# Position bias in whole groups of 16 rows on TensorE, its relus made two groups ahead

## The chip, the cores and the metric

The kernel runs on one core of a Trainium2 chip. The metric is device time in microseconds, the median of several executions. Beside it stands one execution that the hardware profiler recorded: its trace gives the rows below. The engines are called by the profile's names: PE multiplies matrices, PEld loads PE's weights, DVE (vector), ACT (activation) and POOL work elementwise, SP issues most of the transfers.

## The reference, cut to what matters

Attention over 4 batches of 8 heads, 576 positions of 64 features, with a position bias that a small network of 32 hidden units makes; its output goes through two feed-forward stages.

```
scores = q @ k.T / sqrt(64)
rel    = pos[:, None] - pos[None, :]
x      = log1p(|rel|) / log1p(max(pos[:, None], 1))
bias   = relu(x * w1 + b1) @ w2            # one value per head, i and j
attn   = softmax(scores + bias)
x1     = leaky(attn @ v reshaped @ w_in) @ w_out
out    = a routed mixture of 8 experts over x1
```

The bias is the same for all batches. It is 8 x 576 x 576 values, each a sum over 32 hidden units.

## The kernel before

Three phases follow each other. The first one holds the attention, the feed-forward's first product and the position bias, and is the one that the change is in. Its instructions are written in one order and a scheduler then places them on the engines' queues; each engine takes its queue strictly in that order.

**The bias.** A row i of the bias depends on j only through |i - j|, so 16 rows make a group: group m covers rows 16m to 16m+15, and there are 36 groups. `bias_relu` makes for one group four tiles `mk`, one for each q from 0 to 3; each holds 4 rows x 32 hidden units on the 128 partitions and up to 576 distances along the free side. The table `RELU` says for each whether ACT (L222) or DVE (L224) makes it. `bias_units` multiplies each `mk` with the coefficients `cf` (made on POOL, L254) into its own strip of 32 PSUM partitions, `tile_position=(0, 32 * q)` (L270): 4 rows x 8 heads. Four such matmuls, one for each q, are a piece; the 591 columns of a group (576 and 15 for the skewed layout) are cut where the distance turns round and where a PSUM bank ends, two or three pieces in all. Then the strips are copied to the tile `bt` (by ACT, L70, or DVE, L78), and SP writes `bt` to the DRAM tensor `bias` (L284). Up to group 11 and from group 32 on (`both`), all pieces of a group lie in one PSUM tile of the pool `psS`, and one copy takes them; between, each piece has a PSUM tile of the pool `psM`. Both pools have two buffers.

A PE matmul of fp32 data stands in the trace as two records, so a whole piece shows as x8 and a whole group of two pieces as x16; the timeline merges neighbours of one tile under the first one's shape.

**Around it.** `bias_units` is a generator. `phase1` first takes 32 units of it (called the prelude here: groups 0 to 15, with the first loads and conversions of q and k between them), and then the rest comes from a `Filler` between the parts of the first eight attention steps. A step is 128 rows of q of two heads: `scores` (PE L413, then DVE L418, which adds the bias), `exps` (ACT L426), `normalise` (POOL, ACT or DVE, L435 to L444), `transposes` (PE L464, L486) and, at a group's end, `values` (PE L500). From step 8 on the filler gives `up_units` (PE L525, tile `psh`), whose weights `wi` come out of DVE's conversions of `w_in` (`w_t`, L99 to L107, then L78 and L82), spread over the steps from 2 on. Later steps load the bias back from DRAM (`prob<-bias`), and further conversions (`wo_t`) prepare `w_out`.

The filler takes units while a debt is positive, and each unit names its price in ns:

```
quota = 40 * 800.0 / 6.5 if n < 8 else ...
...
fl.run(quota / 2)     # twice in each step
```

Of the kernel before, what the change touches and what calls it, by code (L numbers as in the profile page):

```python
# [38 lines left out]
BC = S + 15  # L39
BP = 608  # L40
# [10 lines left out]

RELU = ("DDAD", "DADD", "DAAD", "ADDA")

WIDE, RELU_BUFS, BIAS_BUFS, COEF_M = 12, 11, 5, 2

PROBS = 4

# [11 lines left out]
def copy_act(nc, out, in_):  # L69
    nc.scalar.activation(out=out, in_=in_, func=AF.Copy)  # L70
# [143 lines left out]
def bias_relu(nc, e, m, qs):  # L214

    out = []
    n = max(16 * m + 16, S - 16 * m)
    for q in qs:
        mk = e.bout.tile([128, S], F32, tag="mk", name="mk", bufs=RELU_BUFS)
        o, x, k = mk[:, :n], e.lw[:, :n], slice(4 * m + q, 4 * m + q + 1)  # L220
        if RELU[m % 4][q] == "A":
            nc.scalar.activation(out=o, in_=x, func=AF.Relu, bias=e.bv[:, k])  # L222
        else:
            nc.vector.tensor_scalar(out=o, in0=x, scalar1=e.bv[:, k], scalar2=0.0, op0=ALU.add, op1=ALU.max)  # L224
        out.append(mk)
    return out


def bias_pieces(m, o):


    c0 = 16 * m + 16
    out = []
    for a, z, d, falls in ((0, c0, c0 - 1, True), (c0, BC, 1, False)):
        while a < z:
            b = min(z, a + 512 - (a + o) % 512)
            out.append((a, b, d, falls))
            d += a - b if falls else b - a
            a = b
    return out  # L240


def bias_units(nc, e, wide):

    nm = S // 16
    nxt = bias_relu(nc, e, 0, range(4))
    for m in range(nm):  # L250
        mk, nxt = nxt, []
        if m % COEF_M == 0:
            cf = e.bout.tile([128, 4 * COEF_M, 4 * H], F32, tag="cf", name="cf", bufs=2)
            nc.gpsimd.tensor_tensor(  # L254
                out=cf, in0=e.coef.rearrange("p g h -> p (g h)").unsqueeze(1).to_broadcast([128, 4 * COEF_M, 4 * H]),
                in1=e.br[:, 4 * m:4 * m + 4 * COEF_M].unsqueeze(2).to_broadcast([128, 4 * COEF_M, 4 * H]), op=ALU.mult,
            )
        bt = e.bout.tile([128, BC], F32, tag="bt", name="bt", bufs=BIAS_BUFS)
        both = m < wide or m >= 32
        o = 0 if m < 4 else 1024 - BC if m >= 32 else 496 - 16 * m  # L260
        pieces = bias_pieces(m, o)
        if both:
            ps2 = e.psS.tile([128, 2, 512], F32, tag="s", name="psb2").rearrange("p a j -> p (a j)")
        half = (len(pieces) + 1) // 2
        for hf in range(2):
            for a, b, d, falls in pieces[half * hf:half * hf + half]:
                ps = ps2[:, o + a:] if both else e.psM.tile([128, 512], F32, tag="m", name="psb")
                for q in range(4):
                    x = mk[q][:, d - (b - a) + 1:d + 1][:, ::-1] if falls else mk[q][:, d:d + b - a]
                    nc.tensor.matmul(  # L270
                        ps[32 * q:32 * q + 32, :b - a], lhsT=cf[:, 4 * (m % COEF_M) + q], rhs=x,
                        start=True, stop=True, tile_position=(0, 32 * q),
                    )
                if not both:
                    (copy_act if hf or m % 2 else copy_dve)(nc, bt[:, a:b], ps[:, :b - a])
            if m + 1 < nm:
                nxt += bias_relu(nc, e, m + 1, (2 * hf, 2 * hf + 1))
            if hf == 1:
                if both:
                    copy_act(nc, bt, ps2[:, o:o + BC])  # L280

                r0 = 16 * (m % 8) * BP
                dst = e.bias_d[m // 8][:, r0:r0 + 16 * (BP + 1)].rearrange("h (r c) -> r h c", c=BP + 1)
                nc.sync.dma_start(out=dst[:, :, :BC], in_=bt)  # L284
            yield 800


class Attention:
# [274 lines left out]
def phase1(ctx, tc, e):  # L563

    nc = tc.nc
# [22 lines left out]
    for k, g in enumerate(groups):  # L588
        b, hf, p = g
# [7 lines left out]
        if hf == 0 and k >= 2:  # L597
            m = n0 - 4 if b == 0 else start[b - 1, 1, p] + 3
# [21 lines left out]

    bias_setup(nc, e)
    bu = bias_units(nc, e, WIDE)
    for k in range(32):
        if k == 20:
            for g in groups[:2]:
                at.q_load(g)
                at.q_hi(g)
                at.q_lo(g)
            for p in range(2):
                at.kv_load(0, p)  # L630
                at.kv_hi(0, p)
                at.k_lo(0, p)
                at.v_load(0, p)
        next(bu)
# [25 lines left out]
    for n, st in enumerate(steps):  # L660
        g = st[:3]
        b, hf, p = g
# [723 lines left out]
def program(tc, e):  # L1386
# [4 lines left out]
    with ExitStack() as top:  # L1391
# [16 lines left out]
        for n, b in (("const", 1), ("big", 1), ("small", 4), ("raw", 1), ("kvp", 1), ("ptp", 1)):  # L1408
            setattr(e, n, pool(wide, n, b, side="right"))
        e.psS, e.psT = (pool(wide, n, 2, space=PSUM) for n in ("psS", "psT"))  # L1410
        tail = phase1(up, tc, e)
        wide.close()

# [60 lines left out]
```

## Time and profile before

| | us |
|---|---|
| median of 3 runs | 1026.42 (1024.62 to 1027.13) |
| the profiled execution, its time | 1025.94 |
| its span (first to last instruction) | 1024.1 |
| PE busy | 980.9 (96%) |
| DVE busy | 680.3 (66%) |
| ACT busy | 545.1 (53%) |
| the 640 records of L270 (position bias on PE), busy | 61.8, from 6.8 to 104 us |

The shares are means over the whole span; the bias stage, the first tenth of it, has its own. Times inside the trace count from the span's start. Busy time of PE is the union of modelled lengths, and a matmul's modelled end lies a little behind the next one's start. The page's "PEclk" is the clock that TensorE was granted, 1.00 for 2.4 GHz and 0.50 for 1.2 GHz.

### The profile page before, as it was taken

To read this page: it belongs to the slowest core of one execution; us is meant where nothing else is said; L and a number is where in the kernel's file an instruction comes from. 1 tells how busy PE (TensorE), PEld (TensorE's weight loads), DVE (VectorE), ACT (ScalarE), POOL (GpSimd) and SP (SyncE) were. 2 spreads that over 40 slices of the span, in tenths; PEclk is the share of its full clock that TensorE was granted. 3 is DMA by queue.
4 is the path that set the end of the run, shared out by engine and by line. 5 is a ranking of instruction groups with operands and counts; after the bars stand their busy time and mean duration, and the time that the engine had idled before them with its cause. 6 is when DMAs were issued, how large, how long until landed. Compare 5 with 4: busy or idle time off the path is not lost.

```text
span 1024.1 us, 19091 instructions
## 1 busy us (share of the span) xinstructions
PE 980.9 (96%) x6294; PEld 807.3 (79%) x6294; DVE 680.3 (66%) x1719; ACT 545.1 (53%) x1102; POOL 101.4 (10%) x112
## 2 busy tenths in 40 slices
PE   5899999999999999999999999999998999999995
PEld 2345778988889988999888888888877888888884
DVE  8888998979865677667766776669983255313312
ACT  5778777546766666555553333344462455424422
POOL 3332421000000000000000000001002111111110
PEclk8999999999999999999999999999999999999998
DMA  7868889989765566545285633437505157312410
GB/s 246 263 201 248 254 282 305 317 269 288 221 205 146 160 188 211 157 141 164 68 259 170 196 113 103 124 117 235 142 21 216 49 198 275 121 42 92 164 41 23
DMA packets 137602, 180.16 MB, mean 176 GB/s; under 512 B 19842, under 2 KB 89858, under 8 KB 137363
## 3 DMA queue, kind: packets, MB, share of 16 engines
q1 hardware_dynamic: 115554, 149.31, 47.4%
q10 hardware_dynamic: 18576, 19.03, 5.3%
q0 software_dynamic: 3360, 10.49, 3.1%
q8 instruction: 52, 0.85, 0.3%
q14 instruction: 60, 0.48, 0.2%
HBM read 196.18 MB, written 43.94 MB: 234 GB/s over the span
## 4 chain that ended last, share of the span: by engine, by line
PE 59%; issue 18%; DMA 12%; DVE 8%; POOL 2%; ACT 1%; SPq 0%; POOLq 0%; DVEq 0%; ACTq 0%
PE psx L784 19%; PE psh L525 15%; PE pss L413 7%; PE psv L500 7%; DMA out_dram<-o,sidx 6%; PE pst L464 5%; PE psb L270 4%; DMA wo_raw<-in_w_out_dram 2%; DVE mk L224 1%; DMA qraw<-in_q_dram 1%; DMA prob<-bias 1%; DVE prob L418 1%; PE psx L486 1%; POOL xg L1241 1%; POOL prob L444 1%
## 5 line engine op out<-in xcount | busy, mean ns | idle before, releaser
L525 PE MATMUL psh<-x,wi 128*128 128x256 f32 (+1 forms) x1536 | 226.8, 298 | 1.7 <-DVE hst L532 1.7
L525 PEld LDWEIGHTS psh<-x,wi 128*128 128x128 f32 x1536 | 211.7, 190 | 3.7 <-DVE hst L532 3.1
L426 ACT ACTIVATE prob<-prob,stat 128x576 f32<-128x576 f32 x144 | 111.3, 773 | 66.4 <-DVE stat L418 55.8
L418 DVE CUSTOM_DVE_ANT_0 prob<-pss,prob 128x576 f32<-128x576 f32 x144 | 107.8, 751 | 22.8 <-PE pss L413 18.7
L784 PE MATMUL psx<-woh,gh 128*128 128x512 f32 x288 | 113.1, 393 | 0.7 <-ACT gh L70 0.7
L784 PE MATMUL psx<-wol,gh 128*128 128x512 f32 x288 | 112.6, 391 | 0.0
L784 PE MATMUL psx<-woh,gl 128*128 128x512 f32 x288 | 112.2, 390 | 0.0
L82 DVE TENSOR_TENSOR htl<-pt,hth 128x512 fp32r<-128x512 f32 x40 | 25.8, 686 | 127.4 <-ACT hth L70 127.4
L70 ACT ACTIVATE gh<-g 128x512 fp32r<-128x512 f32 x72 | 45.4, 632 | 116.4 <-PE psx L784 102.1
L464 PE MATMUL pst<-ident,prob 128*128 128x128 f32 x576 | 89.7, 278 | 4.9 <-DVE pth L78 2.5
L464 PEld LDWEIGHTS pst<-ident,prob 128*128 128x128 f32 x576 | 66.3, 140 | 23.3 <-issue 13.1
L413 PE MATMUL pss<-kt,qhi 128*128 128x288 f32 x256 | 81.7, 334 | 0.0
L1241 POOL DMA_INDIRECT xg<-x,gidx x22 | 23.5, 1067 | 557.6 <-DMA ws<-in_mw_dram 549.0
L270 PE MATMUL psb<-mk,cf 128*32 128x79 f32 (+49 forms) x640 | 61.8, 426 | 12.7 <-POOL cf L254 6.8
L413 PE MATMUL pss<-kt,qlo 128*128 128x288 f32 x256 | 72.6, 298 | 0.0
L500 PE MATMUL psv<-pth,vs 128*64 128x256 f32 (+1 forms) x512 | 71.5, 413 | 0.0
L801 DVE SCALAR_TENSOR_TENSOR junk<-x1s,en 128x512 bf16<-128x512 f32 x96 | 66.0, 687 | 3.5 <-DMA en<-en_d 2.5
L1272 PE MATMUL pu<-w1h,xh 128*128 128x512 f32 x160 | 65.0, 406 | 0.3 <-ACT xh L70 0.3
L70 ACT ACTIVATE pth<-pst 128x512 f32<-128x512 f32 (+1 forms) x100 | 54.5, 549 | 20.1 <-PE pst L464 12.3
L1303 PE MATMUL pd<-w2h,hth 128*128 128x512 f32 x160 | 62.6, 391 | 1.0 <-ACTq L1228 1.0
L784 PEld LDWEIGHTS psx<-woh,gh 128*128 128x128 f32 x288 | 54.1, 188 | 11.8 <-ACT gh L70 1.0
L1272 PE MATMUL pu<-w1l,xh 128*128 128x512 f32 x160 | 63.3, 396 | 0.0
(224 smaller groups left out, 1862.4 us busy)
## 6 DMA issues: line engine op xcount, KB each, us to landing
ws<-in_mw_dram SPq DMA_DIRECT2D x164, 512.0 KB
prob<-bias SPq DMA_DIRECT2D x64, 288.0 KB
g<-h SPq DMA_DIRECT2D x72, 256.0 KB
prob<-bias SPq DMA_DIRECT2D x64, 256.0 KB
bias<-bt SPq DMA_DIRECT2D x36, 295.5 KB
h<-hst ACTq DMA_DIRECT2D x64, 160.0 KB
w_raw<-in_w_in_dram SPq DMA_DIRECT2D x16, 512.0 KB
h<-hst ACTq DMA_DIRECT2D x64, 128.0 KB
```

What stands on the lines that cost most here:

```text
L70: nc.scalar.activation(out=out, in_=in_, func=AF.Copy)
L270: nc.tensor.matmul(ps[32 * q:32 * q + 32, :b - a], lhsT=cf[:, 4 * (m % COEF_M) + q], rhs=x, start=True, stop=True, tile_position=(0, 32 * q),)
L413: nc.tensor.matmul(ps[:, jh, :288], lhsT=lhsT, rhs=kt[:, c0 + 288 * jh:][:, :288], start=(k == 0), stop=(k == len(ops) - 1),)
L418: nc.vector.tensor_tensor_reduce(out=prv, in0=ps[:, :, :288], in1=prv, scale=-0.125, scalar=3.0e38, op0=ALU.add, op1=ALU.min, accum_out=st ...
L426: nc.scalar.activation(out=pr[:, h], in_=pr[:, h], func=AF.Exp, bias=stat[:, 0, h:h + 1], scale=-1.0, accum_out=stat[:, 1, h:h + 1],)
L464: nc.tensor.transpose(ps[:, 128 * c:128 * c + 128], pr[:, h, 64 * h + 128 * c:][:, :128], e.ident)
L500: nc.tensor.matmul(ps[64 * h:64 * h + 64, :n], lhsT=vs[:, c, h], rhs=ph[:, h, c, :n] if c < 4 else pt[:, :n], start=(c == 0), stop=(c == 4 ...
L525: nc.tensor.matmul(ps[:, :n], lhsT=w[:, kc], rhs=x[:, kc, :n], start=(k == 0), stop=(k == 3 * KD - 1),)
L784: nc.tensor.matmul(ps, lhsT=a[:, c % 4], rhs=w[:, c], start=(k == 0), stop=(k == 3 * KF - 1))
L801: nc.vector.scalar_tensor_tensor(out=junk, in0=x1, scalar=1.0, in1=e.en[:, k], op0=ALU.mult, op1=ALU.mult, accum_out=e.dots[:, t, k:k + 1],)
L1272: nc.tensor.matmul(ps, lhsT=a[:, k], rhs=w[:, k, c], start=(i == 0), stop=(i == 3 * KD - 1))
L1303: nc.tensor.matmul(ps, lhsT=a[:, k], rhs=w[:, k], start=(k == 0 and j == 0), stop=(k == 7 and j == 2))
```

## The change

A unit of `bias_units` is a whole group now and is priced at 1600 ns, where it was half of the pieces at 800 ns; the prelude takes 16 units where it took 32, and the loads of q and k stand before the same group, the tenth. The four relus of a group are written as one block, two groups ahead of their matmuls: groups 0 and 1 before the loop, group m+2 behind the matmuls of group m. Before, they were written in two pairs, one behind each half of the group ahead. Eleven buffers for `mk` become 14.

```
--- before.py
+++ after.py
@@ -51,7 +51,7 @@
 
 RELU = ("DDAD", "DADD", "DAAD", "ADDA")
 
-WIDE, RELU_BUFS, BIAS_BUFS, COEF_M = 12, 11, 5, 2
+WIDE, RELU_BUFS, BIAS_BUFS, COEF_M = 12, 14, 5, 2
 
 PROBS = 4
 
@@ -246,9 +246,10 @@
 
 
     nm = S // 16
-    nxt = bias_relu(nc, e, 0, range(4))
+
+    made = [bias_relu(nc, e, m, range(4)) for m in range(2)]
     for m in range(nm):
-        mk, nxt = nxt, []
+        mk = made.pop(0)
         if m % COEF_M == 0:
             cf = e.bout.tile([128, 4 * COEF_M, 4 * H], F32, tag="cf", name="cf", bufs=2)
             nc.gpsimd.tensor_tensor(
@@ -273,16 +274,15 @@
                     )
                 if not both:
                     (copy_act if hf or m % 2 else copy_dve)(nc, bt[:, a:b], ps[:, :b - a])
-            if m + 1 < nm:
-                nxt += bias_relu(nc, e, m + 1, (2 * hf, 2 * hf + 1))
-            if hf == 1:
-                if both:
-                    copy_act(nc, bt, ps2[:, o:o + BC])
-
-                r0 = 16 * (m % 8) * BP
-                dst = e.bias_d[m // 8][:, r0:r0 + 16 * (BP + 1)].rearrange("h (r c) -> r h c", c=BP + 1)
-                nc.sync.dma_start(out=dst[:, :, :BC], in_=bt)
-            yield 800
+        if m + 2 < nm:
+            made.append(bias_relu(nc, e, m + 2, range(4)))
+        if both:
+            copy_act(nc, bt, ps2[:, o:o + BC])
+
+        r0 = 16 * (m % 8) * BP
+        dst = e.bias_d[m // 8][:, r0:r0 + 16 * (BP + 1)].rearrange("h (r c) -> r h c", c=BP + 1)
+        nc.sync.dma_start(out=dst[:, :, :BC], in_=bt)
+        yield 1600
 
 
 class Attention:
@@ -620,8 +620,8 @@
 
     bias_setup(nc, e)
     bu = bias_units(nc, e, WIDE)
-    for k in range(32):
-        if k == 20:
+    for k in range(16):
+        if k == 10:
             for g in groups[:2]:
                 at.q_load(g)
                 at.q_hi(g)
```

How the instructions stand on the queues, at three places. First PE, in the middle of the attention's first eight steps, groups 26 and 27 (`psb` is the bias, x2 or x4 so many of a piece's four matmuls, `pst` the transposes, `pss` the scores). Before:

```order
L270 MATMUL psb<-mk,cf 32x432 x2
L270 MATMUL psb<-mk,cf 32x159 x2
L464 MATMUL pst<-ident,prob 128x128 x3
L270 MATMUL psb<-mk,cf 32x432 x2
L270 MATMUL psb<-mk,cf 32x159 x2
L464 MATMUL pst<-ident,prob 128x128
L413 MATMUL pss<-kt,qhi 128x288
L413 MATMUL pss<-kt,qlo 128x288
L464 MATMUL pst<-ident,prob 128x128 x2
L270 MATMUL psb<-mk,cf 32x448 x2
L270 MATMUL psb<-mk,cf 32x143
L270 MATMUL psb<-mk,cf 32x448
```

With the change:

```order
L271 MATMUL psb<-mk,cf 32x432 x4
L271 MATMUL psb<-mk,cf 32x159 x4
L413 MATMUL pss<-kt,qlo 128x288
L464 MATMUL pst<-ident,prob 128x128 x7
L271 MATMUL psb<-mk,cf 32x448 x4
L271 MATMUL psb<-mk,cf 32x143 x4
```

The pieces of 432 and 159 columns stood there in two halves with three transposes between them, and those of 448 and 143 in three parts; now each group stands in one run.

Second, DVE at the start, behind the seventh relu (`mk` is a relu; `qlo`, `kt` and `w_t` are conversions of q, k and w_in). Before:

```order
L224 TENSOR_SCALAR mk<-lw,v 128x544
L82 TENSOR_TENSOR qlo<-qraw,qhi 128x512
L82 TENSOR_TENSOR kt<-kraw,kt 64x576 x2
L99 TENSOR_SCALAR w_t<-w_raw 128x512
L224 TENSOR_SCALAR mk<-lw,v 128x544
L224 TENSOR_SCALAR mk<-lw,v 128x528 x2
L337 CAST kt<-kt 128x64
L103 SCALAR_TENSOR_TENSOR w_t<-w_raw,w_t 128x512
L99 TENSOR_SCALAR w_t<-w_raw 128x512
L107 SCALAR_TENSOR_TENSOR w_t<-w_raw,w_t 128x512
L224 TENSOR_SCALAR mk<-lw,v 128x512 x2
```

With the change:

```order
L224 TENSOR_SCALAR mk<-lw,v 128x544
L82 TENSOR_TENSOR qlo<-qraw,qhi 128x512
L224 TENSOR_SCALAR mk<-lw,v 128x544
L224 TENSOR_SCALAR mk<-lw,v 128x528
L82 TENSOR_TENSOR kt<-kraw,kt 64x576
L224 TENSOR_SCALAR mk<-lw,v 128x528
L82 TENSOR_TENSOR kt<-kraw,kt 64x576
L224 TENSOR_SCALAR mk<-lw,v 128x512 x2
L337 CAST kt<-kt 128x64
```

The relus of 544 and 528 columns stood behind three conversions and stand behind one; the first steps of `w_t` come after those of 512.

Third, DVE at the end of the prelude, up to the first step's L418, which the order calls ISA. Before:

```order
L224 TENSOR_SCALAR mk<-lw,v 128x384 x3
L224 TENSOR_SCALAR mk<-lw,v 128x368 x3
L78 COPY bt<-psb 128x208
L224 TENSOR_SCALAR mk<-lw,v 128x352
L418 ISA prob,stat<-pss,prob 128x576
L418 ISA stat 128x1
```

With the change:

```order
L78 COPY bt<-psb 128x208
L224 TENSOR_SCALAR mk<-lw,v 128x352
L337 CAST kt<-kt 128x64
L78 CAST wi_77<-w_t 128x4x128
L224 TENSOR_SCALAR mk<-lw,v 128x352
L82 TENSOR_TENSOR wi_78<-w_t,wi_77 128x4x128
L107 SCALAR_TENSOR_TENSOR w_t<-w_raw,w_t 128x512
L224 TENSOR_SCALAR mk<-lw,v 128x336 x2
L78 COPY bt<-psb 128x240
L224 TENSOR_SCALAR mk<-lw,v 128x320 x3
L224 TENSOR_SCALAR mk<-lw,v 128x304 x3
L418 ISA prob,stat<-pss,prob 128x576
```

Between the relus of 368 columns and L418 stood one relu and one copy; now ten relus stand there, a second copy, three conversions that stood further up before (L337, L78 and L82 of `wi`) and one (L107) that stood behind L418.

## Rows read from the trace of the kernel before

**Rows 1.** The page: busy time, share of the span, instructions of each engine.

```profile
PE 980.9 (96%) x6294; PEld 807.3 (79%) x6294; DVE 680.3 (66%) x1719; ACT 545.1 (53%) x1102; POOL 101.4 (10%) x112
```

**Rows 2.** Windows: stretch, busy us PE, PEld, DVE, ACT, POOL, PEclk, DMA, GB/s.

```profile
7.00:33.00 26.00, 20.89 (x214) 9.63 (x214) 25.65 (x50) 17.12 (x30) 9.37 (x12) 0.87 0.82 253
33.00:106.00 73.00, 70.04 (x630) 36.27 (x630) 60.75 (x156) 58.24 (x135) 24.01 (x29) 1.00 0.81 237
90.00:106.00 16.00, 15.23 (x166) 8.78 (x159) 14.86 (x36) 13.82 (x31) 4.96 (x5) 1.00 0.94 272
106.00:120.00 14.00, 13.33 (x103) 11.20 (x101) 13.52 (x34) 9.88 (x24) 4.85 (x5) 1.00 0.84 258
106.00:240.00 134.00, 124.60 (x940) 109.55 (x939) 118.69 (x291) 88.15 (x208) 20.39 (x20) 0.99 0.90 288
160.00:200.00 40.00, 37.77 (x293) 33.83 (x294) 35.77 (x89) 28.53 (x65) 0.75 (x1) 1.00 0.96 315
210.00:215.00 5.00, 5.00 (x28) 4.59 (x30) 3.79 (x10) 3.85 (x9) 0.00 (x0) 0.69 0.83 260
240.00:1024.00 784.00, 765.12 (x4515) 651.66 (x4514) 470.75 (x1212) 379.05 (x731) 45.68 (x43) 1.00 0.47 148
```

**Rows 3.** Waits, 33 to 106 us: us in total, times, longest.

```profile
ACT bt L70 <- PE psb L270: 7.3, 14, 1.6
DVE bt L78 <- PE psb L270: 6.4, 8, 2.2
...
PEld psb L270 <- ACT bt L70: 2.5, 8, 0.7
```

**Rows 4.** Windows, the instructions of psb alone, engines as named there.

```profile
core 0: us, PE busy (x) PEld busy (x) DVE busy (x) ACT busy (x), PEclk, DMA share, GB/s
33.00:106.00 73.00, 40.81 (x426) 14.46 (x426) 5.22 (x10) 15.01 (x35) 1.00 0.81 237
```

**Rows 5.** Timeline of PE: start, length, line, tiles, count.

```profile
66.56 0.58 PE L270 MATMUL psb<-mk,cf 128*32 128x223 f32 x8
...
68.16 1.21 PE L270 MATMUL psb<-mk,cf 128*32 128x384 f32 x16
69.30 0.55 PE L464 MATMUL pst<-ident,prob 128*128 128x128 f32 x3
...
73.89 1.19 PE L270 MATMUL psb<-mk,cf 128*32 128x432 f32 x8
75.01 0.55 PE L464 MATMUL pst<-ident,prob 128*128 128x128 f32 x3
75.49 1.19 PE L270 MATMUL psb<-mk,cf 128*32 128x432 f32 x8
76.61 0.33 PE L464 MATMUL pst<-ident,prob 128*128 128x128 f32 x1
```

**Rows 6.** Timeline of DVE around the end of the prelude.

```profile
25.25 0.41 DVE L78 CAST wi<-w_t 128x512 fp32r<-128x512 f32 x1
...
26.30 0.68 DVE L82 TENSOR_TENSOR wi<-w_t,wi 128x512 fp32r<-128x512 f32 x1
...
32.21 0.19 DVE L337 CAST kt<-kt 128x64 fp32r<-128x64 f32 x1
32.31 0.42 DVE L99 TENSOR_SCALAR w_t<-w_raw 128x512 uint32<-128x512 uint32 x1
...
35.69 0.75 DVE L418 CUSTOM_DVE_ANT_0 prob<-pss,prob 128x576 f32<-128x576 f32 x1
...
40.91 1.60 DVE L224 TENSOR_SCALAR mk<-lw,v 128x304 f32<-128x304 f32 x4
```

**Rows 7.** Timeline of PE in the prelude, with the wait before it.

```profile
13.70 1.19 PE L270 MATMUL psb<-mk,cf 128*32 128x48 f32 x18 [1.69 <-DVE mk L224]
```

**Rows 8.** The chain of waits from 106 to 240 us, by line.

```profile
by line: DMA wo_raw<-in_w_out_dram 13.4%; PE psh L525 11.6%; PE psv L500 10.2%; PE pss L413 8.9%; PE pst L464 7.6%; DMA prob<-bias 7.1%; issue 6.0%; DVE prob L418 5.5%; DMA qraw<-in_q_dram 4.2%; DVE wo_t L103 3.0%; DVE wo_t L107 2.9%; DMA w
```

**Rows 9.** Timeline of PE: the longest wait behind 106 us.

```profile
209.84 1.12 PE L464 MATMUL pst<-ident,prob 128*128 128x128 f32 x4 [2.51 <-DVE pth L78]
```

## The prediction

> **What bounds the kernel now.** I read the page first: PE is busy for 980.9 us of the span, DVE for 680.3 [rows 1]. That is a mean over stages, so I cut the span into stretches [rows 2]. Behind 240 us PE is busy for 765.12 us of 784: from there PE's work sets the end, and what the first 240 us save or lose arrives there in full. The change touches the bias alone, which runs from 6.8 to 104 us, so three stretches matter.
>
> The prelude, 7 to 33 us: DVE is busy for 25.65 us of 26, PE for 20.89 [rows 2]. DVE sets the pace, and PE waits for relus; the longest such wait, 1.69 us, comes before the group at 13.70 [rows 7].
>
> The body, 33 to 106 us, with bias and attention steps mixed: PE 70.04 us of 73, DVE 60.75, ACT 58.24 [rows 2]. PE leads here, and in the list of waits the copies wait for PE, ACT for 7.3 us and DVE for 6.4, while PE's loads wait 2.5 us for ACT's copies [rows 3].
>
> The stretch from 106 to 240 us has no bias. PE is busy for 124.60 us of 134, so 9.4 us are idle, and DVE for 118.69; DMA is busy at 0.90, at 0.96 from 160 to 200 us [rows 2]. In its chain of waits transfers of wo_raw, prob and qraw hold 13.4 + 7.1 + 4.2 = 24.7%, some 33 us [rows 8]. This stretch can swallow a gain.
>
> **The PE term, in the body.** The queue's order shows what becomes of the matmuls: each group's pieces stand in one run, where half of them were torn apart. What a tear costs is seen in the timeline of PE. Groups 23 and 26 have 591 columns each. Group 23, whole, takes from 68.16 to 69.30, 1.14 us. Group 26, in two halves of two strips each, takes 73.89 to 75.01 and 75.49 to 76.61, 1.12 us each: a half costs what a whole does [rows 5], since the strips of a whole piece run side by side. The whole of bias on PE in the body is 40.81 us [rows 4]. The queue before has 35 runs there, and each run's busy time reaches 0.07 us over the start of what follows (1.21 against 1.14): 40.81 - 35 * 0.07 = 38.4 us. The body holds groups 12 to 35 and nearly all of 11, 25 groups; whole, they would take 25 * 1.14 = 28.5 us. So 9.9 us are tears. The order with the change has 24 runs and still tears six pieces (304, 271, 336, 255, 79 and 79 columns); at 1.14 / 591 us a column the second parts cost 1324 * 0.00193 = 2.6 us. PE saves **7.3 us** of work. The number of matmuls, relus and copies stays; nothing is added to an engine.
>
> How much of it moves the end of the body is bounded by DVE. DVE takes over 1.7 us from the prelude (next term), 62.45 us in all. Were all 7.3 us gained, DVE would be busy for 62.45 / 65.7 = 95% of the body. It was at 93% from 90 to 106 us (14.86 of 16) and at 97% from 106 to 120 (13.52 of 14) [rows 2], but in short stretches; over the whole body I take 90 to 93%, which is 69.4 to 67.2 us, a gain of 3.6 to 5.8. I take **4.7 us**; the bounds are 0 (DVE or ACT takes PE's place at once) and 7.3. The nearest row for all of it is the 97%, for none of it the 83% that the body has now.
>
> Here a rule of the Trainium skill speaks against the change. ACT's copies out of PSUM take 15.01 us in the body, DVE's 5.22 [rows 4], and it is they that wait for PE today [rows 3]; ACT would rise from 58.24 of 73 to 58.24 of 68.3 us, 85%, which leaves room. The Trainium skill, "TensorEngine Tiling (Array Packing)", Performance Considerations, says that tiling speeds PE up but not the emptying of PSUM, so that this copy may become the bound. By that rule PE's 7.3 us would turn into waits for buffers, and the sum would be that of the second rival below. The trace so far shows the waits the other way round.
>
> **The DVE term, in the prelude.** On DVE's queue relus move ahead of conversions. Up to the relus of 384 columns the old queue holds one L337, one L99, one L78 and one L82 of wi that the new one does not: 0.19 + 0.42 + 0.41 + 0.68 = 1.7 us [rows 6]. DVE is full there, so the prelude's last relus come up to 1.7 us sooner. The conversions are done later, in the body, where DVE has 73 - 60.75 = 12.25 us idle; without that cover the 1.7 us come back. Bounds 0 and 1.7; I take **1.0**, since PE's four matmuls of the first score, which stood inside group 11, now come behind group 12. Some wait moves with it: the relus of 544 and 528 columns no longer stand behind two kt and one L99, so the 1.69 us in front of 13.70 [rows 7] should shrink; but DVE, not PE, sets the prelude's end, and I add nothing for it.
>
> What becomes late next is the first step. Its L418 began at 35.69 us with 37 relus ahead of it on DVE; now 46 stand ahead. At 1.60 / 4 = 0.40 us each [rows 6] that is 3.6 us more. By the third L418 the count is 52 relus before and 54 after, with two conversions of w_t fewer, so the lag is gone. Behind L418 in each step wait exps, the normalising on POOL and the transposes on PE; PE has bias groups to do meanwhile. I cost it at nothing for that cover; without it, at 3.6 us.
>
> The other edits: three more buffers for mk cost no instruction; the loads of q and k stand before the same group; one cf on POOL per two groups as before (POOL 24.01 us of 73). The unit of 1600 ns for 800 makes the same 20 groups fall into the first eight steps. On SP the loads of vs, qraw and kraw change places with single writes of bias; the stretch from 160 to 200 us, where DMA is fullest, lies well behind. Nothing for these.
>
> **The sum.** 4.7 + 1.0 = 5.7 us by 106 us. Behind it all loads are issued as steps free buffers, so they move with the steps, and DMA has room in the body (0.81 there [rows 2]); but the queue at 0.96 will not take all of it. I let four fifths through: 4.6 us. The profiled execution took 1025.94, so 1021.3; the median of the runs is 0.5 above it: **1021.8 us**. A measurement of this kernel can tell about 0.3%, 3.1 us, from no change, so faster means under 1023.3.
>
> **Rivals.**
> - *All of it arrives, and more* (0.12). 7.3 + 1.7 = 9.0 us: 1017.4. If also the 2.51 us for which PE waits before 209.84 [rows 9], behind which its clock is granted at 0.69 in the mean, so at the lower level for a part [rows 2], fall away, 1014.9. For it speaks that PE is the fullest engine in the body; against it, DVE's 95%.
> - *Gained and given back* (0.28). ACT, DVE or the buffers of PSUM hold the body at its length, or the transfers behind 106 us absorb the shift: 1024 to 1026.4, say 1025.3. For it speaks the chain, with 33 us of landings, and a DVE at 97% from 106 to 120 us; against it, that the loads are tied to the steps.
> - *Slower: the steps lag* (0.14). If not PE's sum but the chain of the eight steps sets the body's end, the late first L418 costs its 3.6 us and the whole pieces nothing gained: 1026.4 + 3.6 = 1030.0. It decides once the steps run out of bias groups before the lag is made up, seen as PE idle between 90 and 106 us well above the 0.77 us of now. Against it: PE is idle for only 3 us in the whole body.
>
> **Chances.** My forecast holds 0.46, its own range 1019 to 1024. A tenth of that ends above 1023.3, a tenth of the second rival below it: faster 0.56, same 0.30, slower 0.14. The range to hold 8 of 10 takes in most of the first rival and of the slower one: 1014.5 to 1029.
>
> **What would show it.** Right: bias on PE in 33 to 106 us near 31 to 33 us busy for 40.81; whole groups as single runs of 1.2 us; the last bias matmul near 98 us for 104; DVE at 90% or more in between; from 240 us the same rows, 4 to 5 us sooner. The prelude term: no wait of 1.69 us before the third group. Wrong: PE busy with bias falls, but the last bias matmul stays at 104 us and PE waits for relus or copies in the body (second rival); or the last bias comes at 98 us and PE's idle time from 106 to 240 rises from 9.4 us by as much; or L418's of the first steps come late and stay late.

## The result, and the profile after

The changed kernel takes 1018.36 us (median of six runs, 1015.72 to 1019.1) beside 1026.29 for the kernel before (six runs, 1024.62 to 1027.26). The ratio is 0.9917, with a 95% interval of 0.9899 to 0.9935: 7.9 us less, beyond the 0.3% that a measurement tells from no change. The number forecast was 1021.8.

The profiled execution of the changed kernel took 1015.88 us, with a span of 1014.0; it is among the two quickest of the six. Profile against profile the gain is 10.1 us, median against median 7.9, and readings from the two traces are to be taken with that difference in mind.

The page's line of busy times after, beside [rows 1]:

```profile
PE 971.1 (96%) x6294; PEld 804.0 (79%) x6294; DVE 680.1 (67%) x1719; ACT 543.5 (54%) x1102; POOL 102.0 (10%) x112
```

As many instructions on every engine, DVE, ACT and POOL as busy as before, PE 9.8 us less busy. The windows after, in the columns of [rows 2]; the stretch from 33 to 93 us is the new body, since the last bias matmul now starts at 93.0 us where it started at 103.4:

```profile
7.00:33.00 26.00, 20.66 (x234) 9.22 (x237) 25.62 (x49) 19.14 (x33) 9.76 (x13) 0.93 0.86 266
33.00:93.00 60.00, 57.59 (x592) 31.00 (x587) 58.19 (x147) 52.53 (x123) 21.07 (x26) 1.00 0.86 256
106.00:240.00 134.00, 125.11 (x943) 110.09 (x942) 116.34 (x293) 87.07 (x208) 16.86 (x16) 1.00 0.90 290
210.00:215.00 5.00, 3.35 (x25) 3.09 (x25) 4.59 (x12) 1.31 (x4) 0.00 (x0) 1.00 0.79 270
```

And the instructions of the bias alone, as in [rows 4]:

```profile
33.00:106.00 73.00, 31.86 (x410) 11.09 (x402) 5.12 (x10) 14.05 (x34) 1.00 0.86 258
```

Bias on PE falls from 40.81 to 31.86 us. In the new body DVE is busy for 58.19 us of 60, 97%, more than PE (57.59); before, PE led and DVE stood at 83%. The prelude looks the same by busy time, DVE 25.62 of 26, and the stretch from 106 to 240 us too: PE idle for 134 - 125.11 = 8.9 us, 9.4 before.

The timeline of PE in the body, group 26 (432 and 159 columns, the group that stood in two halves in [rows 5]) and the group after it:

```profile
68.10 1.20 PE L271 MATMUL psb<-mk,cf 128*32 128x432 f32 x16
69.23 0.40 PE L413 MATMUL pss<-kt,qlo 128*128 128x288 f32 x1
69.47 0.93 PE L464 MATMUL pst<-ident,prob 128*128 128x128 f32 x7
71.67 1.20 PE L271 MATMUL psb<-mk,cf 128*32 128x448 f32 x16 [1.27 <-DVE bt L78]
```

Group 26 is one run and takes 69.23 - 68.10 = 1.13 us, where its two halves took 1.12 each. In front of the next group PE stands 1.27 us for a copy of DVE; before, the longest wait of PE for a copy from 33 to 106 us was 0.3. Who waited for whom from 33 to 106 us, beside [rows 3]:

```profile
PEld psb L271 <- DVE bt L78: 2.3, 3, 1.5
ACT bt L70 <- PE psb L271: 2.1, 4, 1.6
...
PEld psb L271 <- ACT bt L70: 1.8, 6, 0.6
...
PE psb L271 <- DVE bt L78: 1.3, 1, 1.3
```

Before, ACT's copies waited for PE for 7.3 us and DVE's for 6.4; now ACT's wait for 2.1, and of DVE's no wait is left in the list. The other way round PE had waited for copies for 0.7 us in three waits (0.5 for ACT's, 0.2 for DVE's) and now does so once, for the 1.3 us above. PEld's waits for copies went from 2.5 + 1.1 to 1.8 + 2.3 us; one copy can hold up both PE and PEld, so their waits are not to be added. So the copies no longer wait for PE much, and PE waits for copies only a little more.

In the prelude, the wait of 1.69 us in front of the third group [rows 7] is gone, and one of 2.17 us for a copy of ACT stands in front of a later one:

```profile
7.87 5.57 PE L271 MATMUL psb<-mk,cf 128*32 128x16 f32 x66 [0.43 <-DVE mk L224]
15.61 5.07 PE L271 MATMUL psb<-mk,cf 128*32 128x64 f32 x62 [2.17 <-ACT bt L70]
```

Still the last matmul of group 12 starts at 33.5 us, 1.7 us sooner than before (35.2). The first three L418 of DVE's timeline, of which the first stood at 35.69 [rows 6]:

```profile
39.20 0.74 DVE L418 CUSTOM_DVE_ANT_0 prob<-pss,prob 128x576 f32<-128x576 f32 x1
...
41.86 0.76 DVE L418 CUSTOM_DVE_ANT_0 prob<-pss,prob 128x576 f32<-128x576 f32 x1
...
47.15 0.74 DVE L418 CUSTOM_DVE_ANT_0 prob<-pss,prob 128x576 f32<-128x576 f32 x1
```

The first is 3.5 us later than before, the second 1.6 (it stood at 40.23), the third 5.0 sooner (52.12). From there the shift stays: the 17th L418 is 9.5 us sooner, the 61st 9.6 (242.59 to 232.98), the last matmul with w_in starts at 539.8 for 549.5, and the span ends 10.1 sooner.

### The profile page after: what moved, and what is told of

It reads as the page before. It is cut to its first block, busy times and chain, and to the rows that moved or that the text cites. A ratio compares the mean times of both kernels' runs of the same rounds, so it can differ in the third digit from the quotient of the medians.

```text
span 1014.0 us, 19082 instructions
## 1 busy us (share of the span) xinstructions
PE 971.1 (96%) x6294; PEld 804.0 (79%) x6294; DVE 680.1 (67%) x1719; ACT 543.5 (54%) x1102; POOL 102.0 (10%) x112
## 4 chain that ended last, share of the span: by engine, by line
PE 52%; issue 18%; DMA 16%; DVE 9%; ACT 1%; POOL 1%; SPq 1%; POOLq 0%; ACTq 0%; DVEq 0%
PE psx L784 19%; PE psh L525 13%; DMA out_dram<-o,sidx 7%; PE pss L413 6%; PE psv L500 6%; PE pst L464 5%; DVE mk L224 2%; DMA wo_raw<-in_w_out_dram 2%; DMA qraw<-in_q_dram 1%; DMA prob<-bias 1%; PE psb L271 1%; DVE prob L418 1%; DMA w_raw<-in_w_in_dram 1%; DMA w_t<-wo 1%; POOL prob L444 1%
## 5 line engine op out<-in xcount | busy, mean ns | idle before, releaser
L418 DVE CUSTOM_DVE_ANT_0 prob<-pss,prob 128x576 f32<-128x576 f32 x144 | 108.1, 751 | 19.7 <-PE pss L413 16.1
L82 DVE TENSOR_TENSOR htl<-pt,hth 128x512 fp32r<-128x512 f32 x40 | 25.9, 686 | 127.5 <-ACT hth L70 127.5
L271 PE MATMUL psb<-mk,cf 128*32 128x79 f32 (+47 forms) x640 | 52.8, 424 | 14.1 <-POOL cf L255 6.8
L82 DVE TENSOR_TENSOR gl<-g,gh 128x512 fp32r<-128x512 f32 x72 | 49.4, 688 | 21.2 <-ACT gh L70 18.2
```

The lines of the kernel that those rows point to most:

```text
L82: nc.vector.tensor_tensor(out=out, in0=x, in1=hi.bitcast(F32), op=ALU.subtract)
L271: nc.tensor.matmul(ps[32 * q:32 * q + 32, :b - a], lhsT=cf[:, 4 * (m % COEF_M) + q], rhs=x, start=True, stop=True, tile_position=(0, 32 * q),)
L418: nc.vector.tensor_tensor_reduce(out=prv, in0=ps[:, :, :288], in1=prv, scale=-0.125, scalar=3.0e38, op0=ALU.add, op1=ALU.min, accum_out=st ...
```

## The experiments

The theory: a bias piece that is torn into two or more runs costs PE nearly a whole group's time for each, tears come about because its relus are not ready when PE comes to it, and relus made two groups ahead take the tears away; DVE then is the next bound. The rivals: the bigger unit (a whole group between two looks at the attention steps) brings the gain; the three more buffers for `mk` do; or the shift of conversions on DVE does, so that DVE has room still. "Torn" below is counted in the order of PE's queue: the columns of all later parts of a piece, at 1.14 / 591 us each. By that count the kernel before loses 8.3 us in 36 runs of bias matmuls, the changed one 2.4 us in 25. Ratios are to the kernel before, measured beside the experiments: its median was 1025.81 us for `e1` to `e4`, 1026.38 for `e5` to `e8` and 1026.8 for `e9` to `e12`. A ratio can lie 0.001 off that of the two medians. Where two versions are compared that were not measured beside each other, their ratios count for more than their medians.

### The bigger unit alone: relus one group ahead (`e1`)

Of the changed kernel:

```diff
-WIDE, RELU_BUFS, BIAS_BUFS, COEF_M = 12, 14, 5, 2
+WIDE, RELU_BUFS, BIAS_BUFS, COEF_M = 12, 11, 5, 2
-    made = [bias_relu(nc, e, m, range(4)) for m in range(2)]
+    made = [bias_relu(nc, e, m, range(4)) for m in range(1)]
-        if m + 2 < nm:
-            made.append(bias_relu(nc, e, m + 2, range(4)))
+        if m + 1 < nm:
+            made.append(bias_relu(nc, e, m + 1, range(4)))
```

> Half of the change: the unit is a whole group, but the relus are made one group ahead, with 11 buffers. On PE's queue the second parts of torn pieces then come to 9.2 us (8.3 before, 2.4 with the change), so the tears theory expects no gain: 1024 to 1028 us. The rival that the bigger unit itself does it (fewer, longer pieces of filler in the steps) expects nearly all of the change's gain, 1018 to 1020. The rival that DVE's order in the prelude does it (conversions of w_in behind relus) expects no gain either, since that order is the old one here.

Measured: 1027.29 us, ratio 1.0021 (1.0002 to 1.004). Bias on PE in the body, and one group in the timeline:

```profile
33.00:106.00 73.00, 41.82 (x427) 15.52 (x426) 5.21 (x10) 14.82 (x35) 1.00 0.80 232
```

```profile
61.68 1.19 PE L271 MATMUL psb<-mk,cf 128*32 128x368 f32 x4
...
63.16 1.18 PE L271 MATMUL psb<-mk,cf 128*32 128x368 f32 x4
...
64.78 1.19 PE L271 MATMUL psb<-mk,cf 128*32 128x368 f32 x8
```

The pieces of 368 columns are issued as one unit in the program and still stand in three places, each as long as a whole group. Torn: 9.2 us. The bigger unit brings nothing by itself.

### The distance without the bigger unit: halves, two groups ahead, 14 buffers (`e2`)

Of the kernel before:

```diff
-WIDE, RELU_BUFS, BIAS_BUFS, COEF_M = 12, 11, 5, 2
+WIDE, RELU_BUFS, BIAS_BUFS, COEF_M = 12, 14, 5, 2
-    nxt = bias_relu(nc, e, 0, range(4))
+    made = [bias_relu(nc, e, m, range(4)) for m in range(2)]
-        mk, nxt = nxt, []
+        mk, nxt = made.pop(0), []
-            if m + 1 < nm:
-                nxt += bias_relu(nc, e, m + 1, (2 * hf, 2 * hf + 1))
+            if m + 2 < nm:
+                nxt += bias_relu(nc, e, m + 2, (2 * hf, 2 * hf + 1))
             if hf == 1:
+                made.append(nxt)
```

> The other half alone: units stay halves of a group at 800 ns, the relus are made two groups ahead, with 14 buffers. Second parts of torn pieces 1.6 us, DVE's prelude order as with the change. The tears theory expects all of the change's gain or a little more: 1016 to 1019. The unit theory expects the time of before, 1026. The prelude theory expects the change's time, 1018.

Measured: 1014.29 us (four runs), ratio 0.9893 (0.9854 to 0.9931), below all that was expected. In the timeline:

```profile
63.10 1.20 PE L270 MATMUL psb<-mk,cf 128*32 128x384 f32 x16
...
64.87 1.21 PE L270 MATMUL psb<-mk,cf 128*32 128x400 f32 x16
```

Units of halves, yet whole groups on PE: with the relus at hand, the second half follows the first at once. Torn: 1.6 us. The distance of the relus takes the tears away (the three buffers that came with it do little alone, next section), and the bigger unit is not needed. By the medians this version is quicker than the change by 4.1 us, by the ratios by 2.5, with intervals that overlap, so whether it is quicker is not settled. Its trace is 2.6 us shorter than the change's (span 1011.4 for 1014.0), and not in the body, where its last bias matmul comes at 94.9 us, 1.8 later. The windows of this run:

```profile
33.00:93.00 60.00, 57.77 (x574) 29.88 (x566) 56.20 (x145) 51.53 (x122) 22.18 (x26) 1.00 0.85 252
106.00:240.00 134.00, 128.18 (x970) 113.14 (x969) 119.92 (x303) 89.44 (x212) 13.71 (x16) 1.00 0.93 299
```

From 106 to 240 us PE is busy for 128.18 us where the changed kernel has 125.11: 3.1 us of waits less, and its 61st L418 starts at 230.2 us for 233.0. Why the order of this version feeds that stretch better wasn't found.

### The change with 11 buffers (`e3`), the kernel before with 14 (`e4`)

```diff
-WIDE, RELU_BUFS, BIAS_BUFS, COEF_M = 12, 14, 5, 2
+WIDE, RELU_BUFS, BIAS_BUFS, COEF_M = 12, 11, 5, 2
```

and, of the kernel before, the same line the other way.

> The change with 11 buffers for the relus in place of 14: whole units, two groups ahead. Second parts of torn pieces 0.6 us, but on DVE the conversions of kt and wi stand in the prelude as before. The tears theory expects the change's gain or more, less at most 1.7 us for the prelude: 1016 to 1020. The prelude theory expects little or none of it: 1023 to 1026. If the buffers are what counts (relus waiting for PE to free them), also 1023 to 1026.

> The kernel before with 14 buffers and nothing else. Second parts of torn pieces 7.0 us for 8.3. The tears theory expects 1.3 us off, 1024 to 1026; a theory that the buffers count expects 1018 to 1021; unit and prelude theories expect 1026.

Measured: the change with 11 buffers 1020.54 us, ratio 0.9947 (0.9921 to 0.9974), just above the theory's range; the kernel before with 14 buffers 1024.71, ratio 0.9987 (0.9966 to 1.0008). Torn: 0.6 and 7.0 us. Buffers alone take few tears away and bring nothing that can be told from no change. The distance without buffers has fewer tears than the change, but the bias waits longer for DVE's relus. The line of the list of what it waited for over the whole kernel, with 11 buffers:

```profile
  DVE mk L224: 17.0, 26
```

and in the changed kernel, with 14:

```profile
  DVE mk L224: 8.8, 17
```

The list adds the idle time of PE and of PEld, which can be the same wait; PE alone has 6.4 us of it with 11 buffers and 2.8 with 14. A relu made far ahead needs a free buffer to be made into: by the medians some two thirds of the gain (5.3 of 7.9 us) come with the distance and a third with the buffers, though the intervals of the two ratios overlap. The buffers' part is not all in the body: with 11 the last matmul of group 12 starts at 34.9 us, so 1.4 of the prelude's 1.7 us are missing as well.

### Halves with 16 buffers (`e7`), and three groups ahead with 18 (`e12`)

The edits are those of the halves two ahead with 16 for 14 buffers, and with 18 buffers, `range(3)` and `m + 3`.

> The units in halves, relus two groups ahead, with 16 buffers for 14. Second parts of torn pieces 1.3 us for 1.6, runs 24 for 29. If DVE is the bound now, nothing more is to be had from PE's order or the buffers: the time of the 14-buffer version, 1014.3, give or take 1.5. If the buffers still hold relus up (as from 14 to 11), 2 us less: 1012.

> Units in halves, relus three groups ahead, 18 buffers; second parts of torn pieces 1.2 us for 1.6 with two ahead (1014.3) and 2.4 with the change (1018.4). If two groups are already enough to have PE's pieces whole, nothing more comes: 1013 to 1019. If distance still counts: 1010 to 1012. If relus so far ahead keep DVE from the steps' scores: 1020 or more.

Measured: 1018.71 us, ratio 0.9928 (0.9901 to 0.9954), and 1014.49, ratio 0.9884 (0.985 to 0.9917). Torn: 1.3 and 1.2 us. Three ahead equals two ahead (1014.29). With two more buffers at the same distance the median is 4.4 us higher, above both times that were expected, though a few tears less are left; by the ratios it is 3.6 us, and the intervals overlap, so this cost is not settled either. From 106 to 240 us PE is busy for 126.46 us there, for 127.98 three ahead. So once the tears are gone, what still differs may lie in the stretch behind the bias and in the order of the queues there, not in the tears. That is left open.

### Copies put on DVE, read from `lw` (`e5`, `e6`)

Two copies of 576 columns in each of the first seven steps, of the kernel before and of the changed one:

```diff
+    bl = e.bout.tile([128, S], F32, name="bl")
+        if n < 7:
+            for _ in range(2):
+                nc.vector.tensor_copy(bl, e.lw)
```

> The kernel before with 14 more copies of 128x576 on DVE (two in each of the first seven attention steps, from one SBUF tile into another that nobody reads), some 14 * 0.45 = 6 us of work that is no part of the computation. DVE is busy for 83% of the body before, with 12 us idle. If PE bounds the body there, the copies hide: 1024 to 1028 us. If DVE already bounds it, 1030 to 1033.

> The changed kernel with the same 14 copies. Second parts of torn pieces stay at 1.8 us for 2.4. In its trace DVE is busy for 97% of the body. Theory: with the tears gone the bound has passed from PE to DVE, so the copies show at nearly their full 6 us: 1022.5 to 1025. Rival: PE still leads and the 97% only runs beside it: 1018 to 1020.

Measured: 1026.53 us, ratio 1.0 (0.9982 to 1.0019), and 1017.55, ratio 0.9909 (0.9877 to 0.9941). On the kernel before 14 * 0.45 = 6.3 us of copies are hidden; on the changed one too, against the theory's expectation. The copies' own row in the second run says why that isn't the body's answer:

```profile
L684 DVE COPY bl<-lw x14: 432/452/920, 6.8 to 97.4; 128x576 f32<-128x576 f32 x14
```

They depend on nothing but `lw`, so the scheduler put 6 of the 14 ahead of 33 us, the first at 6.8 us, and the load that was to fall into the body fell into the start. The pair tells little of the body, and was made again with copies that can't move up.

### Copies on DVE tied to the steps (`e9`)

Of the changed kernel, four in each of the first seven steps, reading that step's scores:

```diff
+            for _ in range(4):
+                nc.vector.tensor_copy(bl, at.prob[st][0][:, 1])
```

> The earlier 14 copies could be taken by DVE long before the step they stood in (6 to 8 of them before 33 us), so they did not test the body. Here the changed kernel has 28 copies of 128x576 on DVE, four in each of the first seven steps, that read the step's own probabilities and so can't run before it: 28 * 0.45 = 12.6 us of work that is no part of the computation. Torn pieces as with the change (2.4 us). If DVE bounds the body now (97% busy, 2 us idle): 8 to 12 us more, 1026 to 1030. If PE still does: up to 3 us more, 1018 to 1021.

Measured: 1027.57 us, ratio 1.0004 (0.9982 to 1.0025).

```profile
33.00:93.00 60.00, 56.15 (x487) 27.18 (x483) 57.48 (x147) 46.25 (x110) 19.77 (x25) 0.97 0.76 221
```

```profile
L684 DVE COPY bl<-prob x28: 432/449/924, 47.8 to 105.8; 128x576 f32<-128x576 f32 x28
```

DVE stays at 57.48 us of 60, and the copies push its other work out: the last bias matmul moves from 93.0 to 101.7 us, and 28 * 0.45 = 12.6 us of copies cost 9.2 (8.9 by the ratios). ACT is down to 46.25 of 60. DVE has next to no room left in the new body. The same copies weren't run on the kernel before, and they stand in the chain of their steps, so that some of the 9.2 us may be the steps' wait for them; and the granted clock of this stretch is 0.97 in this trace, 1.00 in the changed kernel's.

### Bias matmuls made twice (`e10`, `e11`)

Of the changed kernel and of the kernel before, the matmuls of six groups doubled:

```diff
-                for q in range(4):
+                for q in list(range(4)) * (2 if m >= 12 and m % 4 == 0 else 1):
```

> The changed kernel with the matmuls of groups 12, 16, 20, 24, 28 and 32 made twice into the same place: 6 * 1.14 = 6.8 us more on PE, nothing more elsewhere, the output unchanged. If DVE bounds the body now, PE has little room too (96% busy with waits inside), but the work falls into waits: 0 to 3 us more, 1018 to 1021. If PE bounds it: all of it, 1024 to 1026.

> The kernel before with the same groups made twice: 6.8 us more on PE. The order then tears far fewer pieces (second parts about 2.5 us for 8.3), so the tears theory expects a wash: 6.8 less 5.8, 1026 to 1029 us, though PE has 24 more matmuls. A theory in which tears don't matter and PE bounds the body expects 1031 to 1034; one in which DVE's order is all that counts expects 1025 to 1027.

Measured: 1021.5 us, ratio 0.9959 (0.9938 to 0.998), and 1028.86, ratio 1.0022 (1.0006 to 1.0038). The bias alone on PE, the first of the changed kernel with doubled groups, the second of the kernel before with them:

```profile
33.00:106.00 73.00, 38.15 (x514) 13.77 (x506) 5.18 (x10) 14.19 (x34) 1.00 0.86 261
```

```profile
33.00:106.00 73.00, 39.00 (x530) 15.25 (x530) 5.15 (x10) 14.81 (x35) 1.00 0.85 253
```

On the changed kernel the bias grows by 38.15 - 31.86 = 6.3 us, of which 3.1 arrive in the time by the medians, 4.3 by the ratios, between the two times that were expected: PE is still part of the bound, with a third to a half of what is put on it hidden, where of DVE's copies about a quarter was. On the kernel before, six groups more *lower* the bias's time, from 40.81 to 39.00 us: while PE is held by the second matmuls the relus get ahead of it, and few pieces are torn. Those 6.8 us of work (six groups at 1.14) cost 2.1. A tear is thus a matter of how far the relus stand ahead of PE, as the theory has it.

### A fourth of some groups' relus on POOL (`e8`)

Of the halves two ahead:

```diff
-RELU = ("DDAD", "DADD", "DAAD", "ADDA")
+RELU = ("DDAD", "DADP", "DAAD", "ADDA")
+        elif RELU[m % 4][q] == "P":
+            nc.gpsimd.tensor_scalar(out=o, in0=x, scalar1=e.bv[:, k], scalar2=0.0, op0=ALU.add, op1=ALU.max)
```

> The units in halves, relus two groups ahead, 14 buffers, and one relu of every 16 (nine in all) on POOL in place of DVE: 9 * 0.46 = 4 us off DVE, at some 1 us each on POOL, which is busy for a third of the body. Second parts of torn pieces 3.0 us for 1.6. If DVE bounds the body: 2 to 4 us less than 1014.3, so 1010 to 1012. If POOL's relus come late for PE, or hold up the normalising that POOL also does: 1015 to 1019.

Measured: 1021.88 us, ratio 0.9967 (0.995 to 0.9984), 7.6 us above the same kernel without it and above both times that were expected. POOL's row of them:

```profile
L224 POOL TENSOR_SCALAR mk<-lw,v 128x560 f32<-128x560 f32 (+8 forms) x9 | 18.7, 2079 | 5.5 <-DVE v L203 3.6 <-PE psb L272 1.8
```

Nine relus at 2.08 us each, where DVE's 90 in the halves two ahead take 0.37 to 0.92, 0.46 in the median: they come late, the torn parts rise from 1.6 to 3.0 us, the last matmul of group 12 starts at 35.1 us (33.4 without it) and the last bias matmul at 98.3. Work taken from DVE did not help here, since it was made late.

## Why the prediction was right, and by how much it missed

The mechanism held. The time came out 3.4 us below the number and just below the forecast's own range (1019 to 1024), inside the range to hold 8 of 10; it lies 1.0 above that of the first rival ("all of it arrives"), which had a chance of 0.12. The two terms that held gain back, DVE's share in the body and the four fifths behind it, were not borne out.

- *Tears on PE*: 7.3 us of work less were predicted, with 31 to 33 us of bias in the body. Measured: 31.86, and behind group 12 38.6 to 30.9 us, 7.7 less. The tears were put a little high: 9.9 and 2.6 us were predicted, 8.3 and 2.4 is the count of the queues, whose difference is 5.9. Eleven runs fewer, with 0.07 us of overlap each, make another 0.8; the last 1.0 of the 7.7 us is assigned to neither. The runs with one group ahead and with doubled matmuls show that it is the tears, and the relus' distance that takes them away.
- *What of it moves the body's end*: this term was mis-sized. 4.7 us were let through, since DVE's share was set at 90 to 93%. DVE ran at 97% for 60 us. The prediction took the 97% from 106 to 120 us for a short stretch's, and left out here that its own row of the prelude has DVE busy for 25.65 us of 26, 99% [rows 2]. From group 12's last matmul to the last bias matmul the body shrank from 68.2 to 59.5 us, by 8.7. With the 17th L418's shift of 9.5 us as the measure, less the prelude's 1.7 if all of that lasts, 7.8 of it is gain that lasts: all of PE's 7.7. The bounds of 0 and 7.3 held but for 0.5; the choice between them failed.
- *Prelude*: predicted 1.0 of at most 1.7, measured 1.7. The wait of 1.69 us went as said and another of 2.17 for ACT's copy came, at no cost that shows: DVE, busy for 25.62 us of 26, paces that stretch. The granted clock there was 0.87 before and is 0.93 now, but it isn't what moved the prelude's end: with one group ahead it was 1.00, and group 12's last matmul started at 35.4 us.
- *The first step's L418*: 3.6 us later was predicted, caught up by the third; measured 3.5, 1.6, then 5.0 sooner. The cover held, and the slower rival had no ground.
- *The way from 106 to 240 us*: four fifths were let through; 9.3 us at the first matmul with w_in (111.9 to 102.6 us) became 9.6 at the 61st L418. All of it passed, with the transfers' queue as full as before (0.90). That the loads' tie to the steps carried it is the prediction's reason, and no run tests it.
- *The second rival* fell: of its waits PE has one of 1.3 us for a copy in the body and one of 2.2 in the prelude, and the body ends some 10 us sooner all the same. The prediction set it beside a rule of the Trainium skill ("TensorEngine Tiling (Array Packing)", Performance Considerations), that the copy out of PSUM may become the bound; the trace shows the rule in those two waits and not in the time. What bounds the body now is not one engine alone: of what was put on DVE nearly three quarters arrived in the time, of what was put on PE a half to two thirds. DVE's part is all its work, and its copies out of PSUM are 5.1 us of that.
- *The clock*: 210 to 215 us has a granted clock of 1.00 for 0.69, and the wait of 2.51 us [rows 9] has become two of 1.11 and 1.65; PE's idle time from 106 to 240 us fell by 0.5 us only, and from the 17th to the 61st L418 both kernels take about as long (140.7 and 140.5 us), so this part of the first rival gave little.

The 9.5 us at the 17th L418 are 10.1 at the end of the two profiles, and the medians differ by 7.9. The six executions of the change lie 3.4 us apart, and its profile is one of the quickest; so the terms above, read from the two traces, add up to some 2 us more than the medians show. In several other traces (the halves with 14, 16 and 18 buffers, the 11 buffers, the relus on POOL) there is a stretch near 760 to 775 us with windows of 5 us at a granted clock between 0.5 and 0.85, which neither profile of the pair has. That such stretches make the spread is not shown: the halves with 14 buffers have one in the quickest of their four executions. What stays open besides is whether the change and its form in halves differ, by 2.5 to 4 us, and why.

## What to carry to other kernels

Where matmuls on some strips of PE run side by side, count the runs in PE's queue, not the matmuls: a part of a torn piece can cost a whole one's time (here 1.12 us for 1.14), and what helped here was to have its inputs ready sooner (distance and buffers together), not a bigger unit in the program. When the leading engine gives up work, look up the highest share that the trace shows the next one to sustain anywhere (DVE 99% in the prelude and 97% from 106 to 120 us here, and 97% in the body afterwards) before you take a cautious middle. A test load must depend on something of the stretch that it is to load, or the scheduler may put it elsewhere.

## What the runs showed of the hardware

- More matmuls took PE less time: with six groups doubled the kernel before was busy with bias for 39.00 us from 33 to 106 us, for 40.81 without (the whole kernel took 2.1 us longer).
- A relu of 304 to 560 columns took POOL 2.08 us in the mean of nine; DVE's 90, of 304 to 576 columns, take 0.46 us in the median.
- In the body of the changed kernel DVE was busy for 58.19 us of 60 and PE for 57.59 at once.
